# Three order changes in a fused attention and MLP training kernel: squares into the oldest output slots, one turned r tile behind the merged matrix's fourth block, two r stores moved

## The chip, the cores and the metric

The kernel runs on one core of a Trainium2 chip. The metric is the device time of one execution in microseconds (us); lower is better. A core has five engines with a queue each, and each takes its instructions in order: TensorE (PE, matmuls; PEld is its weight load), VectorE (DVE), ScalarE (ACT), GpSimd (POOL) and SyncE (SP). SP, ACT and POOL also issue DMA transfers, and an issue that waits holds up what stands behind it in the same queue. Accumulators of matmuls are in PSUM, all other tiles in SBUF.

## The reference

The reference is a transformer block with linear attention and a gated MLP, and its gradients: it returns the output and the gradients of the input and of five weight matrices. The tensors are bf16; x is 1 x 2048 x 640, there are 32 heads of 20 columns, and the MLP is 1728 wide.

```python
def _A_ref(x, wqkv, wo):
    ...
    q, k, v = qkv[0], qkv[1], qkv[2]
    phi = lambda t: jnp.where(t > 0, t + 1, jnp.exp(t)) + 1e-6
    pq, pk = phi(q), phi(k)
    kv = jnp.einsum("bhsd,bhse->bhde", pk, v)
    z = jnp.einsum("bhsd->bhd", pk)
    num = jnp.einsum("bhqd,bhde->bhqe", pq, kv)
    den = jnp.einsum("bhqd,bhd->bhq", pq, z)[..., None] + 1e-6
    o = num / den
    return (lambda x, *d: x.transpose(*d))(o, 0, 2, 1, 3).reshape(B, S, D) @ wo
...
x = A_x
h = x + _A_ref(_layernorm(x, axis=-1), A_wqkv, A_wo)
h2 = h + _B_ref(_layernorm(h, axis=-1), B_w1, B_w3, B_w2)
...
_out, _vjp = jax.vjp(_f, A_x, A_wqkv, A_wo, B_w1, B_w3, B_w2)
_grads = _vjp(grad_out)
```

## The kernel before

The 2048 rows are 16 tiles of 128 rows (index t), the 640 columns five blocks of 128 (index m or i). The order of instructions on every engine is the order of the program text: it is written out by hand, and waits between engines follow from which tile is read and written. A buffer with a tag and a number of copies is handed out in turn, and a new tile in it waits for the last reader of the old one.

*First part (to about 98 us).* The kernel forms the normalised x, the query features pq and the key features pk. Instead of kv it forms a merged matrix m = (normalised x) against pk, in five blocks: `m_part` adds matmuls (L430), `m_end` casts a finished block to SBUF with ACT (L437) and, for the first four blocks, turns it into `mT` by a DMA transpose on SP (L442). `kvT_block` (L449) multiplies mT with the value weights; for m = 2 it reads columns 240 to 400 of mT, the last 16 of which come from the fourth block. For each row tile the kernel forms r, the query features divided by their denominator: `r_prod` (POOL for tiles 0 to 7, L367), `r_red` (DVE, L374), `r_inv` (DVE) and `r_scale` (DVE, L381). `r_row` is the last three of these, and `r_head` is `r_row` and then `r_T`, which turns the tile into pqT by a DMA transpose on SP (L385). r also goes to DRAM, for the backward part: `r_store` issues that on POOL (L735).

The query tiles 0 to 3, 8 and 9 lie in one large tile (hx in the profile); tiles 4 to 7 lie in `pql`, a tag with four copies. After tile 7 the next to take a copy of it are `f2_hn(2)`, the normalised h of row tile 2 (in the place of tile 4), and the load `r_load(8)` (in the place of tile 5), issued on SP (L740).

The list in `run(...)` (from L947 on) gives the order of the end of this part. `f2_wT` makes the matrix Wp, turned by five DMA transposes on SP (L709). `f2_half` multiplies turned r with Wp into `at` (L657), adds it to x and takes the statistics on DVE; POOL forms the reciprocal root by a power (L155); `f2_hn` writes the normalised tile hn on DVE (L161); for tiles 2 and 3 PE transposes hn (L768, `trh`). `f2_m_out` stores the merged matrix's fifth block from POOL (L715).

*Middle.* The MLP, its backward part and the attention's backward part follow; the change does not touch them.

*Value gradient (about 560 to 611 us).* `obs` is an output tile of 128 x 3200, used as a ring. Gradient jobs (`grad_halves`, L1344) take slots of 320 columns in turn by a counter, ten in all: ACT casts the accumulator into the slot (L1348) and POOL stores it (L1350). Jobs 0 to 9 of the query gradient come first; `fill(1)` issues half a job. Into the last loops five "squares" are mixed, one for each block of the value weight gradient: `square` forms it (L1378), `unload` copies columns 0 to 379 with ACT and 380 to 639 with DVE (L1384) into a piece of 640 columns of obs (two slots of a job), and POOL stores it (L1455). The squares come at n = 8, 10, 12, 14 and 16 of the loop; by the first of them jobs 0 to 7 are cast and half of job 8 is issued. Accumulators of squares and of the matmuls around them (L1439, `dkv`) share three buffers.

Of the kernel before, what the change touches and what calls it, by code (L numbers as in the profile page):

```python
# [55 lines left out]
def kernel(  # L56
# [20 lines left out]
    dma, dmaT, dmaG = SY.dma_start, SY.dma_start_transpose, G.dma_start  # L77

    def rows(ap):
        return ap.rearrange("(t p) d -> p t d", p=P)  # L80
# [22 lines left out]
    r_v, pk_v, xn_v, hn_v, m_v, pq_v = rows(r_d), rows(pk_d), rows(xn_d), rows(hn_d), rows(m_d), rows(pq_d)  # L103
# [149 lines left out]
    def p1_tr(t, parts=((0, DT),)):  # L253
        xn = x_sb[:, t, :]
        for a, b in parts:
            tr = ps.tile([P, DT, P], BF16, name="tr", bufs=2)
            for c in range(a, b):
                T.transpose(tr[:, c, :], xn[:, c * P:(c + 1) * P], ident[:])

            A.copy(out=pqT[:, a:b, t * P:(t + 1) * P], in_=tr[:, a:b, :])  # L260
# [13 lines left out]
    def p1_mm(t, n0, between=None, halves=None):  # L274
        acc = p1_acc() if halves is None else None
        for j in range(2):
            p1_half(acc[:, j, 0:HD] if halves is None else halves[j][:, 0:HD], t, n0 + j * HD)
            if j == 0 and between is not None:
                between()
        return acc  # L280
# [22 lines left out]
    def phi_rest(keep=0):  # L303
        while len(held) > keep:
            held.pop(0)()

    pqs = {}
# [13 lines left out]
    def q_tile(t):  # L321
        q_home(t)
        phi(p1_mm(t, 0), pqs[t], t)
# [7 lines left out]
    def z_diag(m):  # L331
        dz[m] = hx[:, 10, m * P:(m + 1) * P]
        V.tensor_scalar(out=dz[m], in0=ident[:], scalar1=Z[:, m:m + 1], scalar2=None, op0=ALU.mult)
# [25 lines left out]
    def r_prod(t):  # L359
        for j in range(2):  # L360
            js = slice(j * HD, (j + 1) * HD)
            if t < 8:
                pr[t, j] = (p1.tile([P, HD], F32, name="pr", bufs=2) if t % 2 else
                            pf.tile([P, HD], F32, name="pr", tag="h2", bufs=2))[:]
            else:
                pr[t, j] = ps.tile([P, 512], F32, name="prp", tag="at", bufs=2)[:, 0:HD]
            (G if t < 8 else V).tensor_tensor(out=pr[t, j], in0=pqs[t][:, js], in1=Zb[:, js], op=ALU.mult)  # L367
# [4 lines left out]
    def r_red(t, js=(0, 1)):  # L372
        for j in js:
            V.reduce_sum(out=rden[:, t, j * 16:(j + 1) * 16], in_=heads(pr.pop((t, j))), axis=AX.X)  # L374

    def r_inv(t):
        V.tensor_scalar(out=rden[:, t, :], in0=rden[:, t, :], scalar1=1e-6, scalar2=None, op0=ALU.add)
        V.reciprocal(out=rden[:, t, :], in_=rden[:, t, :])

    def r_scale(t):  # L380
        V.tensor_tensor(out=heads(pqs[t]), in0=heads(pqs[t]),  # L381
                        in1=rden[:, t, :].unsqueeze(2).to_broadcast([P, H, DH]), op=ALU.mult)

    def r_T(t):
        dmaT(out=pqT[:, :, t * P:(t + 1) * P], in_=pqs[t])  # L385
# [39 lines left out]
    def m_part(m, tiles, js=(0, 1)):  # L425
        if m not in macc:
            macc[m] = [ps.tile([P, 512], F32, name="macc", tag=("m", "tr")[m % 2], bufs=2) for _ in range(2)]
        for t, j in [(t, j) for t in tiles for j in js]:
            n = HD + (m < 2) * j
            T.matmul(macc[m][j][:, 0:n], lhsT=pk_all[:, t, m * P:(m + 1) * P],  # L430
                     rhs=x_ext[:, t, j * HD:j * HD + n], start=(t == 0), stop=(t == ST - 1))

    def m_end(m, js=(0, 1)):
        mb = mbs[:, m % 4, :]
        acc = macc[m]
        for j in js:
            A.copy(out=mb[:, j * HD:(j + 1) * HD], in_=acc[j][:, 0:HD])  # L437
        if m < 2:
            A.copy(out=Z[:, m:m + 1], in_=acc[1][:, HD:HD + 1])
            z_diag(m)  # L440
        if m < DT - 1:
            dmaT(out=mT[:, :, m * P:(m + 1) * P], in_=mb)  # L442
# [13 lines left out]
    def load_w2T(a, b):  # L456
        dmaT(out=w2T[:, :, a:b], in_=B_w2[a:b, :])
# [70 lines left out]
    for t in range(ST):  # L528
        first = None
        if t < RAW:  # L530
# [11 lines left out]
            k = p1_mm(t, D, between, kh)  # L542
            act(0, 1)
            act(1, 1)
        else:
            k = p1_mm(t, D, (lambda: p1_tr(t + 1)) if t + 1 < XT_DMA else None)
# [30 lines left out]
    def r_row(t):  # L577
        r_red(t)
        r_inv(t)
        r_scale(t)  # L580

    def r_head(t):
        r_row(t)
        r_T(t)
# [24 lines left out]
    phi_rest()  # L609
    m_part(3, range(5))  # L610
    q_tile(6)
    r_head(1)
    r_prod(3)
    phi_rest()
    m_part(3, range(5, 11))
# [4 lines left out]
    phi_rest()  # L620
    m_part(3, range(11, ST))
    m_end(3)
    r_T(2)
    load_w2T(4 * P, 8 * P)
    dmaG(out=m_v[:, 1:4, :], in_=mbs[:, 1:4, :])
# [4 lines left out]
    kvT_block(1, big())  # L630
    r_row(4)
    r_prod(6)
    phi_rest()
    m_part(4, range(5, 11))
    q_tile(9)
# [308 lines left out]
    def kv3():  # L944
# [5 lines left out]
        (f2_wT, 4), (phi_rest,), (q_late, 14), (r_T, 4), (r_head, 5), (load_x, 4, 6), (r_prod, 7),  # L950
        (q_out, 10, 14), (mlp_ghh, 4),
        (q_late, 15), (w2_room,), (sig_table,), (f2_half, 0, 0), (f2_half, 1, 0), (f2_half, 2, 0), (f2_half, 3, 0), (mlp_ghh, 5),
        (f2_half, 0, 1), (r_store, 4, 5), (f2_half, 1, 1), (f2_hn, 0), (r_store, 5, 6), (f2_half, 2, 1), (f2_hn, 1),
        (f2_half, 3, 1), (f2_m_out,),
        (f2_half, 4, 0, True), (mlp_ghh, 6), (f2_half, 4, 1, True), (f2_half, 5, 0, True), (r_red, 6, (0,)), (f2_hn, 2), (f2_hn, 3),
        (f2_ht, 2), (f2_ht, 3), (load_w2T, 8 * P, 10 * P), (mlp_ghh, 7), (r_red, 6, (1,)), (r_inv, 6), (r_scale, 6),
        (r_T, 6), (f2_rest,), (r_red, 7), (r_inv, 7), (r_scale, 7), (r_T, 7), (r_store, 6, 7))
# [38 lines left out]
    for c in range(SC):  # L996
# [9 lines left out]
        for fc in range(FT):  # L1006
# [23 lines left out]
            if c == SC - 1 and fc in (1, 2, 5, 6):  # L1030
                i = (1, 2, 5, 6).index(fc)
# [339 lines left out]
    def d_acc():  # L1371
        return ps.tile([P, 2, 512], F32, name="dkv", bufs=3)

    def square(lhsT, rhs, i):

        acc = d_acc()
        for c, a, b, bank, off, first in SQ:
            T.matmul(acc[:, bank, off:off + (b - a) * DH], lhsT=lhsT[:, c, i * P:(i + 1) * P],  # L1378
                     rhs=rhs[:, c, a * DH:b * DH], start=first, stop=True, skip_group_check=True)
        return acc  # L1380

    def unload(acc, out):
        for bank, (a, b) in enumerate(((0, SPLIT_D), (SPLIT_D, H))):
            (A.copy, V.tensor_copy)[bank](out=out[:, a * DH:b * DH], in_=acc[:, bank, 0:(b - a) * DH])  # L1384

    def fill(n):
        for _ in range(n):
            next(jobs, None)
# [45 lines left out]
    for n in range(0, SC * DT, 2):  # L1434
        pair = [divmod(i, DT) for i in (n, n + 1)]
        acc = d_acc()
        for b, (c, d) in enumerate(pair):
            for k in range(DT):
                T.matmul(acc[:, b, :], lhsT=gm[:, k, d * P:(d + 1) * P], rhs=xnT[c][:, k, :], start=(k == 0),  # L1439
                         stop=(k == DT - 1))  # L1440
        for b, (c, d) in enumerate(pair):
            cs = slice(c * W, (c + 1) * W)
            pm = dx.tile([P, W], BF16, name="pm", bufs=2)
            V.tensor_scalar(out=pm[:], in0=pkT[:, d, cs], scalar1=1.0, scalar2=None, op0=ALU.min)
            V.scalar_tensor_tensor(out=g_kT[:, d, cs], in0=acc[:, b, :], scalar=gz[:, d:d + 1], in1=pm[:], op0=ALU.add,
                                   op1=ALU.mult)
        if n < 16:
            fill(1)
        if 8 <= n < 8 + 2 * DT:
            i = n // 2 - 4  # L1450
            sq = square(mN, gkv_b, i)
            k = (4, 0, 1, 2, 3)[i]
            ob = obs[:, k * D:(k + 1) * D]
            unload(sq, ob)
            dmaG(out=out2S[:, i, 2 * D:3 * D], in_=ob)  # L1455
# [21 lines left out]
    def both_grads(m, f0, f1):  # L1477

        return [(max(f0, lo) - f0, min(f1, lo + F) - f0, out[:, m, max(f0, lo) - lo:min(f1, lo + F) - lo])
                for lo, out in ((0, out4S), (F, out5S)) if max(f0, lo) < min(f1, lo + F)]  # L1480
# [60 lines left out]
    for i, (f0, f1) in enumerate(blocks):  # L1541
        n = f1 - f0
        for m in range(DT):
            last = (i, m) == (len(blocks) - 1, DT - 1)
            for a, b in ((0, n - P), (n - P, n)) if last else ((0, n),):
                c = (a + b) // 2
                halves = ((a, c), (c, b)) if i * DT + m < 6 else ((a, b),)
                out = [(x + y - a, z + y - a, to) for y, w in halves for x, z, to in both_grads(m, f0 + y, f0 + w)]
# [43 lines left out]
```

## Time and profile before

| what | us |
|---|---|
| median of 3 runs | 821.31 (820.56 to 822.07) |
| the profiled execution | 819.31 |
| its span, first to last instruction | 817.3 |
| PE busy in the span | 812.6 |
| PE busy in the window 90 to 100 | 9.98 |
| PE busy in the window 595 to 612 | 17.00 |

The granted TensorE clock is 1.00 in all windows. The span is what the trace shows; the execution's own time is 2.0 us longer. The timeline gives, for each group of like instructions that follow each other, the start in us, the time they cover, the engine, the line, the operation, what is written and read, shapes and the number; in square brackets stands how long the engine was idle just before and what ended it.

### The profile page before, as it was taken

The numbers are of one execution on the slowest core, as the hardware profiler recorded it, in microseconds if no ns is written. First come the engines' busy times: TensorE is split into PE (matmuls) and PEld (weight loads), VectorE is DVE, ScalarE is ACT, GpSimd is POOL, SyncE is SP. The second block draws the span as 40 slices with busy tenths as digits, with TensorE's granted clock in tenths as the row PEclk, the third lists the DMA queues.
The fourth block names the chain that finished last, engine by engine and source line by source line (L and its number), as shares of the span: only waits on it lengthen the run. The fifth ranks groups of instructions, "written<-read, shape, count | busy, mean of one in ns | idle before, by whom it ended". The sixth has DMA issues, their size and how long they took to land.

```text
span 817.3 us, 13571 instructions
## 1 busy us (share of the span) xinstructions
PE 812.6 (99%) x5227; PEld 495.2 (61%) x5227; DVE 444.9 (54%) x976; ACT 324.4 (40%) x607; POOL 128.6 (16%) x194
## 2 busy tenths in 40 slices
PE   9999999999999999999999999999999999999998
PEld 6777544555555555754577777777657777544444
DVE  7859997998898566300057777772565551000000
ACT  7856688665565666011122212222113442111111
POOL 2243333323222212100001111110120000000000
PEclk9999999999999999999999999999999999999999
DMA  9799899696485556999867887259995679679991
GB/s 257 210 241 283 207 264 317 203 243 175 125 211 154 169 173 168 227 263 239 242 176 182 211 198 199 58 114 180 214 184 104 122 166 255 177 179 233 239 220 38
DMA packets 334480, 159.83 MB, mean 196 GB/s; under 512 B 252304, under 2 KB 327920, under 8 KB 334416
## 3 DMA queue, kind: packets, MB, share of 16 engines
q1 hardware_dynamic: 290976, 119.37, 62.7%
q0 software_dynamic: 7008, 23.17, 8.4%
q10 hardware_dynamic: 36432, 16.42, 8.2%
q8 instruction: 41, 0.67, 0.3%
q14 instruction: 23, 0.19, 0.1%
HBM read 44.47 MB, written 53.43 MB: 120 GB/s over the span
## 4 chain that ended last, share of the span: by engine, by line
PE 98%; DVE 1%; ACT 0%; DMA 0%; POOL 0%; issue 0%
PE mm L395 21%; PE job L1344 20%; PE ghn L1131 14%; PE gxn L1495 8%; PE gw L1086 7%; PE big L268 4%; PE o L913 4%; PE o L859 3%; PE gwo L1219 3%; PE macc L430 3%; PE at L657 3%; PE gr L1188 3%; PE dkv L1439 3%; PE mm L268 1%; PE dkv L1378 1%; PE gp L395 1%
## 5 line engine op out<-in xcount | busy, mean ns | idle before, releaser
L1344 PE MATMUL job<-gb,g_q 128*128 128x496 bf16 (+3 forms) x576 | 116.8, 366 | 0.0
L1131 PEld LDWEIGHTS <-ggb 128*128 128x128 bf16 x864 | 84.5, 98 | 33.0
L395 PE MATMUL mm<-pqT,w 128*128 128x512 bf16 x405 | 93.6, 379 | 0.0
L1344 PEld LDWEIGHTS <-g_q 128*128 128x128 bf16 x576 | 55.8, 98 | 61.0
L395 PEld LDWEIGHTS <-w 128*128 128x128 bf16 x540 | 52.6, 98 | 63.0 <-issue 0.8
L1348 ACT CAST obs<-job 128x496 bf16<-128x496 f32 (+4 forms) x56 | 28.6, 511 | 136.5 <-PE job L1344 126.0
L1131 PE MATMUL ghn<-w13a,ggb 128*128 128x320 bf16 x448 | 63.5, 299 | 0.0
L1131 PE MATMUL ghn<-w13b,ggb 128*128 128x320 bf16 x416 | 61.4, 299 | 0.0
L1146 DVE SCALAR_TENSOR_TENSOR wb<-gs,hnb 128x640 f32<-128x640 bf16 x16 | 13.2, 825 | 88.1 <-ACT gs L1143 88.1
L395 PE MATMUL mm<-g2T,w2T 128*128 128x512 bf16 x240 | 59.6, 379 | 0.0
L1086 PE MATMUL gw<-hb,g 128*128 128x512 bf16 (+2 forms) x320 | 58.6, 346 | 0.0
L1086 PEld LDWEIGHTS <-g 128*128 128x128 bf16 x320 | 31.3, 98 | 26.9
L420 ACT CAST ghh<-mm 128x512 bf16<-128x512 f32 x48 | 28.1, 585 | 47.6 <-PE mm L395 41.2
L1196 POOL TENSOR_TENSOR sz<-Zb,g_h 128x640 f32<-128x640 bf16 x16 | 20.2, 1261 | 163.6 <-DVE g_h L1197 163.6
L796 ACT ACTIVATE sig<-mm 128x512 bf16<-128x512 f32 x56 | 33.7, 602 | 25.2 <-PE mm L395 21.7
L1143 ACT ACTIVATE gs<-ghn 128x640 bf16<-128x640 f32 x16 | 11.2, 703 | 77.1 <-PE ghn L1131 77.1
L395 PEld LDWEIGHTS <-w2T 128*128 128x128 bf16 x260 | 25.4, 98 | 23.4
L268 PEld LDWEIGHTS <-pqT 128*128 128x128 bf16 x320 | 30.7, 98 | 13.5 <-ACT pqT L260 0.9
L1344 PEld LDWEIGHTS <-g 128*128 128x128 bf16 x320 | 31.0, 98 | 12.8
L268 PE MATMUL big<-wqkv,pqT 128*128 128x320 bf16 x250 | 38.5, 299 | 0.2
L832 DVE TENSOR_TENSOR gate<-gate,sig 128x1024 bf16<-128x1024 bf16 x28 | 19.3, 689 | 33.8 <-ACT gate L807 31.1
L1091 ACT CAST gw2o<-gw 128x512 bf16<-128x512 f32 (+2 forms) x20 | 10.4, 519 | 65.5 <-PE gw L1086 25.5
(212 smaller groups left out, 1378.1 us busy)
## 6 DMA issues: line engine op xcount, KB each, us to landing
hh_d<-hhT SPq DMA_DIRECT2D x24, 256.0 KB, 2.8
gg_d<-gate POOLq DMA_DIRECT2D x24, 256.0 KB, 4.4
gg_d<-ghh POOLq DMA_DIRECT2D x24, 256.0 KB, 4.1
ggb<-gg_d SPq DMA_DIRECT2D x6, 896.0 KB, 5.4
ggb<-gg_d ACTq DMA_DIRECT2D x6, 832.0 KB, 5.6
ggb<-gg_d SPq DMA_DIRECT2D x2, 1728.0 KB, 12.6
x_sb<-in_A_x_dram SPq DMA_DIRECT2D x4, 640.0 KB, 5.1
pk_d<-pk_all SPq DMA_DIRECT2D x4, 640.0 KB, 5.7
```

The costliest lines, as they stand in the source:

```text
L268: T.matmul(acc, lhsT=pqT[:, c, t * P:(t + 1) * P], rhs=wqkv[:, c, n0:n0 + HD], start=(c == 0), stop=(c == DT - 1))
L395: T.matmul(acc[:], lhsT=w[:, c, fc * P:(fc + 1) * P], rhs=rhs[:, c, :], start=(c == 0), stop=(c == DT - 1))
L420: A.copy(out=ghh[n // 2][:, n % 2, :], in_=acc[:])
L430: T.matmul(macc[m][j][:, 0:n], lhsT=pk_all[:, t, m * P:(m + 1) * P], rhs=x_ext[:, t, j * HD:j * HD + n], start=(t == 0), stop=(t == ST - 1))
L657: T.matmul(at[:, 0:HD], lhsT=pqT[:, c, t * P:(t + 1) * P], rhs=Wp[:, c, j * HD:(j + 1) * HD], start=(c == 0 and not on_pe), stop=(c == DT ...
L796: A.activation(sig[:, i, :], gp[:], AF.Sigmoid)
L913: T.matmul(o2["ps"][:, 0:HD], lhsT=hhT[c][:, fc, i * P:(i + 1) * P], rhs=w2[:, fc, j * HD:(j + 1) * HD], start=(fc == 0), stop=(fc == FT - 1))
L1086: T.matmul(acc[:, 0:fw], lhsT=g2[:, t, m * P:(m + 1) * P], rhs=hb[b][:, t, 0:fw], start=(t == 0), stop=(t == ST - 1))
L1131: T.matmul(acc[:, j, 0:HD], lhsT=ggb[t // 2][:, k, lo:lo + P], rhs=rhs[:, j * HD:(j + 1) * HD], start=(k == 0), stop=(k == NG - 1))
L1344: T.matmul(acc[:, 0:n], lhsT=lhs[:, t, m * P:(m + 1) * P], rhs=rhs(t), start=(t == 0), stop=(t == ST - 1))
L1348: A.copy(out=ob, in_=acc[:, 0:n])
L1495: T.matmul(acc[:, j, 0:HD], lhsT=g, rhs=wqT[:, k, j * HD:(j + 1) * HD], start=(k == 0), stop=(k == 14))
```

## The change

- `r_head(1)` becomes `r_row(1)`, and `r_T(1)` comes after `m_end(3)`. On SP, the transpose of r tile 1 and that of the merged matrix's fourth block change places; nothing else moves in that queue.
- The store of r tile 4 moves up on POOL, to behind the products of tile 6. It is issued by a line of its own, as `r_store` is not defined yet there.
- The store of r tile 5 moves down, to behind the store of the merged matrix's fifth block.
- The five squares take the pieces 0, 1, 2, 3, 0 of obs; before they took 4, 0, 1, 2, 3.

```diff
@@ first part @@
     m_part(3, range(5))
     q_tile(6)
-    r_head(1)
+    r_row(1)
     r_prod(3)
...
     m_end(3)
+    r_T(1)
     r_T(2)
     load_w2T(4 * P, 8 * P)
...
     r_row(4)
     r_prod(6)
+    dmaG(out=r_v[:, 4, :], in_=pqs[4])
     phi_rest()
...
-        (f2_half, 0, 1), (r_store, 4, 5), (f2_half, 1, 1), (f2_hn, 0), (r_store, 5, 6), (f2_half, 2, 1), (f2_hn, 1),
-        (f2_half, 3, 1), (f2_m_out,),
+        (f2_half, 0, 1), (f2_half, 1, 1), (f2_hn, 0), (f2_half, 2, 1), (f2_hn, 1),
+        (f2_half, 3, 1), (f2_m_out,), (r_store, 5, 6),
@@ value gradient @@
             i = n // 2 - 4
             sq = square(mN, gkv_b, i)
-            k = (4, 0, 1, 2, 3)[i]
+            k = i % 4
             ob = obs[:, k * D:(k + 1) * D]
             unload(sq, ob)
             dmaG(out=out2S[:, i, 2 * D:3 * D], in_=ob)
```

## The prediction, made before the changed kernel was run

> **What bounds the kernel now.** I began with the page: the busy times and the chain that ended last.
>
> ```profile
> span 817.3 us, 13571 instructions
> PE 812.6 (99%) x5227; PEld 495.2 (61%) x5227; DVE 444.9 (54%) x976; ACT 324.4 (40%) x607; POOL 128.6 (16%) x194
> ...
> PE 98%; DVE 1%; ACT 0%; DMA 0%; POOL 0%; issue 0%
> ```
>
> TensorE (PE) is busy for all but 4.7 us (817.3 - 812.6), and the chain that ends the run is PE for 98% of the span. So time can be won only where a matmul waits. The second view is the list of waits on PE alone (engine, line, what released it: sum, times, longest).
>
> ```profile
> PE warm L468 <- DVE zero L125: 1.1, 1, 1.1
> PE k L268 <- DMA wqkv<-in_A_wqkv_dram: 0.5, 2, 0.3
> ```
>
> Both belong to the first microseconds, which the change does not touch. But matmul ends are modelled, so a short wait can hide inside a busy PE. I therefore read the timeline at each of the places the change touches, from start to start: matmuls of 320 columns follow each other every 0.136 us (ten in 1.36 us in the chain), of 512 columns every 0.216 us.
>
> First, the stores of turned r rows (L735) and the normalised tiles (hn):
>
> ```profile
> 91.99 0.59 POOL L735 DMA_DIRECT2D r_d<-pql  x1
> ...
> 94.63 0.48 DVE L374 TENSOR_REDUCE rden<-pr 128x16 f32<-128x320 f32 x1
> 94.82 0.84 PE L657 MATMUL at<-Wp,pqT 128*128 128x320 bf16 x5
> 95.18 0.82 DVE L161 TENSOR_SCALAR hn<-x_sb,ln_mv,ln_rs 128x640 bf16<-128x640 bf16 x2
> 95.69 0.82 PE L768 MATMUL trh<-ident,hn 128*128 128x128 bf16 x10
> ```
>
> The five matmuls from 94.82 are over at 94.82 + 5 x 0.136 = 95.50, and the transposes of hn start at 95.69: PE stands for 0.19 us. hn of tile 2 lies in the buffer that held tile 4's r row, so it waits for that row's store. Second, the value-gradient squares and the output slots (obs):
>
> ```profile
> 601.09 0.42 ACT L1348 CAST obs<-job 128x320 bf16<-128x320 f32 x1 [4.95 <-DMA out_dram<-obs]
> ...
> 601.41 0.48 ACT L1384 CAST obs<-dkv 128x380 bf16<-128x380 f32 x1
> ...
> 601.93 0.43 DVE L1384 CAST obs<-dkv 128x260 bf16<-128x260 f32 x1 [2.37 <-ACT obs L1384]
> ...
> 602.62 1.24 PE L1439 MATMUL dkv<-xnT,gm 128*128 128x512 bf16 x5
> ```
>
> ACT stands 4.95 us for the store of the first square, since a later cast wants half of its slot; the second square is unloaded behind it, and its accumulator is taken again by the matmuls at 602.62. They come 0.26 us after the unload's end (601.93 + 0.43 = 602.36): PE loses nothing, by 0.26 us. Third, the queue of transposes on SP:
>
> ```profile
> 67.65 2.45 SPq L385 DMA_TRANSPOSE pqT<-hx  x1
> ...
> 70.20 1.24 SPq L442 DMA_TRANSPOSE mT<-hx  x1
> ...
> 75.39 1.12 PE L449 MATMUL kv<-mT,wqkv 128*128 128x160 bf16 x15
> ```
>
> Landings come from the DMA view, asked for each issue alone (KB, us from issue to landing): the L735 store at 91.99, the first square's store at 596.89, mT's fourth block at 70.20, the third Wp transpose at 82.29.
>
> ```profile
> r_d<-pql POOLq DMA_DIRECT2D x1, 160.0 KB, 3.1
> ```
>
> ```profile
> out_dram<-obs POOLq DMA_DIRECT2D x1, 160.0 KB, 4.1
> ```
>
> ```profile
> mT<-hx SPq DMA_TRANSPOSE x1, 4.8
> ```
>
> ```profile
> Wp<-pkx SPq DMA_TRANSPOSE x1, 2.7
> ```
>
> So r's store lands at 95.1 (hn starts 0.08 later), the square's at 601.0 (the cast starts 0.09 later), mT's block at 75.0 (0.39 before its first reader at 75.39), Wp's third block at 85.0 (0.20 before the first at matmul, 85.19).
>
> **The change, part by part.** No matmul, vector operation or byte is added or removed; PE's order is the same. It moves three DMA issues and five slot numbers.
>
> *Store of r tile 4, earlier.* It goes from POOL at 91.99 to behind the products of tile 6 (issued 73.06 for 1.53 us), where it waits for the scaling of tile 4 on DVE (74.31 + 0.97 = 75.28) and takes 0.59 us of POOL. Queued behind it on POOL is the product of tile 7, which starts at 84.16: 8.3 us of cover, cost 0. What it frees: hn of tile 2 no longer waits for a landing at 95.1. DVE is next late, since its queue holds the reduction until 94.63 + 0.48 = 95.11: gain 95.18 - 95.11 = 0.07 us. Bounds: 0, and 0.28, the whole of the gap (0.19) and of the one behind the next five matmuls (96.35 + 5 x 0.216 = 97.43 to 97.52, 0.09). I take 0.07.
>
> What it costs where it goes: 160 KB join a full stretch (DMA share 1.00 between 75 and 90). Over the run POOL's queue moved 23.17 MB in 8.4% of 817.3 us, so 160 KB are 0.49 us of all 16 engines. It would land near 75.3 + 3.1 = 78.4, before the first Wp transpose is issued (79.67), with the 640 KB x load between them. The third Wp has 0.20 us to spare, so the loss lies between 0 and, if 0.49 us passed through whole, 0.29. I take 0, nearer to the row: this transpose took 2.7 us where the least of the five took 2.6, so its issue and not the backlog sets it.
>
> The Trainium skill (DMA: Bandwidth & Descriptors, section SWDGE vs HWDGE vs iDMA) says that the two kinds of queue feed different internal queues of each DMA engine, which takes them in turn. By that rule a transpose under way would give up every other turn to the store, and its delay ends with the store's own 0.49 us; the sum would then hold up to +0.29. The rows are harsher: the transpose at 67.65 ran beside a 480 KB POOL store and took 7.1 us, where the one at 71.54 took 4.0.
>
> *Store of r tile 5, later.* From POOL at 93.12 to behind the store of mT's fifth block (95.30 + 0.58 = 95.88). The next POOL work is the power for tile 4 at 100.22: 3.7 us of cover. Its buffer is next written by a load that SP issues at 111.92; landing near 95.9 + 3.0 = 98.9 leaves 13 us. Both stores also leave the row of power operations on POOL (92.60, 93.73), but DVE's hn of tile 1 (93.44) follows its own previous step at 93.38 at once, so nothing is won. Cost 0.
>
> *r_T(1) behind mT's fourth block, on SP.* Each issue keeps its work; the two change places. mT's source is cast by 65.71 + 0.75 = 66.46, so it can go out at 67.65 instead of 70.20. In r_T(1)'s place (7.1 us) it would land at 74.75 rather than 75.0; if it kept its own 4.8 us, at 72.45. kv starts at 75.39 behind matmuls, so 0 is won here and the margin grows from 0.39 to between 0.64 and 2.9 us. r_T(1) lands near 75.0; its reader, tile 1's at matmuls, starts at 85.87 (85.19 + 5 x 0.136): 10.9 us of cover. r_T(2) and all behind keep their places. Cost 0.
>
> *Squares in slots 0 to 3, then 0.* The cast no longer waits for the square's store: ACT and DVE run some 2 us sooner at 601, and PE gains 0, as it did not wait. The new waits: squares 0 to 3 now go where jobs 0 to 7 were, whose last store is issued at 592.81, 13 us before square 3's unload (606.39). Square 4 needs square 0's store, landed at 601.0, before its unload at 608.88: 7.9 us. Cost 0.
>
> Sum: the profiled execution took 819.31 us (span 817.3 and 2.0 around it), so 819.31 - 0.07 = 819.24. The median of the three runs is 821.31, 2.00 above the profiled execution, and the page does not say where those 2.00 us go.
>
> **What the landings add.** An estimate: the four L735 stores of this profile took 3.1, 3.0, 2.1 and 5.3 us. hn starts at DVE's own pace if the landing takes at most 3.03 (so that it is back at DVE by 95.11); the mean of what lies above it is (0.07 + 0 + 0 + 2.27) / 4 = 0.59 us. The change takes that wait away. For the median I so take 821.31 - 0.59 = 820.7. The other two (slack of 0.26 and 0.39 us) get nothing in it.
>
> **The rivals.**
>
> *All of the 2.00 us are such waits* (hn's store, the square's store, mT's block). For it: of the three landings one decides a start and two come within 0.4 us; the rows of these transfers spread widely (mT 3.3 to 7.4 us, obs stores 2.0 to 6.5). A landing of 5.3 at hn costs 2.2 us, of 6.5 at the square 6.5 - 4.1 - 0.26 = 2.1, of 7.4 at mT 7.4 - 4.8 - 0.39 = 2.2. Against: the profile shows none of it. Then 821.31 - 2.00 - 0.07 = 819.2.
>
> *The moved store delays Wp: slower.* The 480 KB beside the 67.65 transpose went with 3.1 us more (7.1 against 4.0). If 160 KB did as much to the third Wp transpose, PE would stand before the first at matmul for 3.1 - 0.20 = 2.9 us: 824.2. It is slower by over 0.2% from a delay of 1.84 us (0.20 + 1.64). Against: a third of the bytes, and the x load between them.
>
> *It does nothing*: PE is full and every piece lies in cover. 821.2.
>
> **How the numbers follow.** 0.2% is 1.64 us, about what a measurement of this kernel can tell from no change. Chances: the forecast 0.38, nothing 0.12, all waits gone 0.34, Wp delayed 0.16. The first two are within 0.2%: same 0.50; faster 0.34; slower 0.16. The time is 820.7, the forecast's. The range goes from 818.9, just below the 819.2 of the rival, to 822.8, past which lies most of the slower case (its partial stalls, such as 0.49 or 1 us, are inside). The forecast's own range is 820.0 to 821.6.
>
> **What would show it.** In the profile after: hn of tile 2 starts right behind the reduction on DVE, and the gap before the hn transposes falls to about 0.12 us; the wait of obs L1348 on its store is gone and the ACT cast comes near 599; mT's fourth block is issued at about 67.6 and r_T(1) at about 70.2; the at matmuls follow the queries without a gap at 85.2. I am wrong if PE stands before the first at matmul, if the store on POOL holds up tile 7's product, or if repeated runs fall by more than 1.6 us while the profile shows no wait removed.

## The result, and the profile after

The changed kernel took 819.35 us (median of 14 runs, 819.10 to 820.21), the kernel before 820.74 us in the 14 runs beside it (819.39 to 822.24). The ratio is 0.9982, 95% interval 0.9974 to 0.9991: 1.5 us less, between 0.7 and 2.1. That is clear of no change, though just inside the 0.2% that the prediction called the same.

The profiled execution of the changed kernel took 819.31 us, to a hundredth what the profiled one of before took. From the page, its span, the busy times and the chain:

```profile
span 817.4 us, 13576 instructions
...
PE 811.9 (99%) x5227; PEld 494.9 (61%) x5227; DVE 445.1 (54%) x976; ACT 324.7 (40%) x607; POOL 129.0 (16%) x194
...
PE 98%; DMA 1%; ACT 0%; SPq 0%; issue 0%
```

The list of PE's waits after:

```profile
PE warm L468 <- DVE zero L125: 1.1, 1, 1.1
PE k L268 <- DMA wqkv<-in_A_wqkv_dram: 1.1, 2, 0.6
PE tr L258 <- ACT x_sb L479: 0.2, 1, 0.2
PE mm L395 <- DMA pqT<-hn: 0.2, 1, 0.2
```

One execution against one execution so shows no gain at all: the loads of the first microseconds cost 0.6 us more here (1.1 against 0.5), and the list has a wait that was not in that of the kernel before, for the DMA transpose of hn. Three timelines show what the change did. Around hn:

```profile
94.53 0.48 DVE L374 TENSOR_REDUCE rden<-pr 128x16 f32<-128x320 f32 x1
...
94.79 0.84 PE L659 MATMUL at<-Wp,pqT 128*128 128x320 bf16 x5
94.93 0.97 DVE L161 TENSOR_SCALAR hn<-x_sb,ln_mv,ln_rs 128x640 bf16<-128x640 bf16 x2
95.19 0.58 POOL L717 DMA_DIRECT2D m_d<-hx  x1
...
95.47 0.93 PE L770 MATMUL trh<-ident,hn 128*128 128x128 bf16 x10
...
95.77 0.54 POOL L737 DMA_DIRECT2D r_d<-pql  x1
...
96.24 1.24 PE L395 MATMUL mm<-g2T,w2T 128*128 128x512 bf16 x5
...
97.64 0.61 PE L395 MATMUL mm<-pqT,w 128*128 128x512 bf16 x2 [0.15 <-DMA pqT<-hn]
```

From the end of the at matmuls to the first mm there were 96.35 - 95.50 = 0.85 us; now there are 96.24 - (94.79 + 0.68) = 0.77. That is 0.08 less, about the 0.07 of the prediction, though in another way: the gap before the hn transposes is gone, and the ten transposes take 0.77 us instead of 0.66. But the next matmuls begin at 97.64, where 96.24 + 5 x 0.216 = 97.32 would do: 0.32 us of wait in place of 0.09. Around the second square, ACT no longer waits for a store:

```profile
599.07 0.42 ACT L1350 CAST obs<-job 128x320 bf16<-128x320 f32 x1 [2.73 <-PE job L1346]
599.44 0.47 ACT L1386 CAST obs<-dkv 128x380 bf16<-128x380 f32 x1
...
599.95 0.43 DVE L1386 CAST obs<-dkv 128x260 bf16<-128x260 f32 x1 [0.23 <-ACT obs L1386]
```

The square is unloaded at 600.38 (before, 602.36), and PE takes its accumulator at 602.77: the slack of 0.26 us has become 2.4. And the first square's store, which landed in 4.1 us in the profile of before, took longer in this execution (DMA view, that issue alone, at 597.10):

```profile
out_dram<-obs POOLq DMA_DIRECT2D x1, 160.0 KB, 5.4
```

With the old slots, an estimate: 5.4 us instead of 4.1 would have cost 5.4 - 4.1 - 0.26 = 1.0 us of PE. On SP, the merged matrix's block goes out sooner:

```profile
67.85 2.46 SPq L442 DMA_TRANSPOSE mT<-hx  x1
70.42 2.54 SPq L385 DMA_TRANSPOSE pqT<-hx  x2
```

### The profile page after: what moved, and what is told of

The parts are those of the page before. It is cut to its first block, busy times and chain, and to the rows that moved or that the text cites. A ratio compares the mean times of both kernels' runs of the same rounds, so it can differ in the third digit from the quotient of the medians.

```text
span 817.4 us, 13576 instructions
## 1 busy us (share of the span) xinstructions
PE 811.9 (99%) x5227; PEld 494.9 (61%) x5227; DVE 445.1 (54%) x976; ACT 324.7 (40%) x607; POOL 129.0 (16%) x194
## 4 chain that ended last, share of the span: by engine, by line
PE 98%; DMA 1%; ACT 0%; SPq 0%; issue 0%
PE mm L395 21%; PE job L1346 20%; PE ghn L1133 14%; PE gxn L1497 8%; PE gw L1088 7%; PE big L268 4%; PE o L915 4%; PE o L861 3%; PE gwo L1221 3%; PE macc L430 3%; PE gr L1190 3%; PE dkv L1441 3%; PE at L659 3%; PE mm L268 1%; DMA wqkv<-in_A_wqkv_dram 1%; PE dkv L1380 1%
```

## The experiments

Each kernel was timed beside the kernel before on the same chip; times are medians, "before" is that of its group. The first is the kernel before itself and the last differs from the changed kernel; all others differ from the kernel before by the edit shown.

| kernel | us | before | ratio (95% interval) |
|---|---|---|---|
| before, again | 820.43 | 820.56 | 0.9998 (0.9990 to 1.0007) |
| squares alone | 819.54 | 820.56 | 0.9989 (0.9980 to 0.9998) |
| turn alone | 820.35 | 820.56 | 1.0001 (0.9993 to 1.0009) |
| stores alone | 820.37 | 820.56 | 0.9999 (0.9990 to 1.0008) |
| turn and stores | 821.15 | 821.09 | 1.0003 (0.9993 to 1.0014) |
| squares and stores | 819.75 | 821.09 | 0.9985 (0.9977 to 0.9994) |
| squares, worse slots | 821.31 | 821.09 | 1.0005 (0.9994 to 1.0016) |
| stores swapped | 821.00 | 821.09 | 1.0002 (0.9991 to 1.0013) |
| cast later | 820.24 | 821.52 | 0.9987 (0.9974 to 0.9999) |
| stores late | 822.27 | 821.52 | 1.0014 (0.9999 to 1.0030) |
| squares and turn | 820.23 | 821.52 | 0.9985 (0.9973 to 0.9996) |
| changed, two stores later still | 820.30 | 821.52 | 0.9986 (0.9975 to 0.9997) |

### One part at a time

**The kernel before, again** (no edit).

> The kernel before, again. Every theory: ratio 1.000 to the kernel before, within 0.1%; it shows the noise of the comparison. Its executions should spread over some 3 us as before (819.4 to 822.2). The profile may catch another execution than the first one: if landings decide, the three places (hn of tile 2 after the r store, the cast behind the first square's store, kv after mT's fourth block) are where PE then stands.

It came out the same, 0.9998. Its profile caught another execution (820.0 us), in which mT's fourth block landed late:

```profile
PE kv L449 <- DMA mT<-hx: 0.9, 1, 0.9
```

The block was issued at 70.41 and took 5.8 us, so it landed at 76.2; kv began at 76.23, where 75.19 (ten matmuls from 73.83, 0.136 us each) would have done. PE stood there for 0 us in one profiled execution of this program and for 1.0 us in the other.

**Squares alone.**

```diff
-            k = (4, 0, 1, 2, 3)[i]
+            k = i % 4
```

> Only the squares' slots are changed (0, 1, 2, 3, 0). Theory (the store of r tile 4 holds up hn): within 0.3 us of the kernel before, with its spread of 3 us. Rival A (the cast that waits for the first square's store is what costs in repeated runs): 1.0 to 1.5 us faster, 819.3, with a spread of 1 us. Rival B (mT's fourth block): no change.

0.9989: 0.9 us, and the interval leaves out no change. That is rival A's direction, a little under its size, with a spread of 1.6 us (819.06 to 820.64) where 1 was expected; the kernel before beside it spread over 3.7 us (819.01 to 822.74).

**Turn alone.**

```diff
-    r_head(1)
+    r_row(1)
...
     m_end(3)
+    r_T(1)
     r_T(2)
```

> Only the transpose of r tile 1 is put behind mT's fourth block. Theory (r store of tile 4): within 0.3 us of the kernel before. Rival A (squares): no change. Rival B (mT's fourth block comes late for kv in repeated runs): 1.0 to 1.5 us faster, 819.3, with a spread of 1 us.

1.0001: rival B falls as the main cause. The wait at kv is there, but it shows in one of the nine profiles without the turn.

**Stores alone.**

```diff
     r_prod(6)
+    dmaG(out=r_v[:, 4, :], in_=pqs[4])
...
-        (f2_half, 0, 1), (r_store, 4, 5), (f2_half, 1, 1), (f2_hn, 0), (r_store, 5, 6), (f2_half, 2, 1), (f2_hn, 1),
-        (f2_half, 3, 1), (f2_m_out,),
+        (f2_half, 0, 1), (f2_half, 1, 1), (f2_hn, 0), (f2_half, 2, 1), (f2_hn, 1),
+        (f2_half, 3, 1), (f2_m_out,), (r_store, 5, 6),
```

> Only the stores of r tiles 4 and 5 are moved. Theory (hn of tile 2 waits for the landing of r tile 4's store): 0.6 to 1.4 us faster, 819.4 to 820.1, with a narrower spread. Rivals A and B: within 0.3 us of the kernel before.

0.9999: the theory of the prediction falls as the main cause; the interval leaves it 0.8 us at most. The profile of this run, which has the old slots, shows in its place what squares cost. PE's rows around the second and third squares:

```profile
604.01 0.49 PE L1379 MATMUL dkv<-gkv_b,mN 128*128 128x140 bf16 x6
604.88 0.81 PE L1440 MATMUL dkv<-xnT,gm 128*128 128x512 bf16 x3 [0.38 <-DVE obs L1385]
```

The six short matmuls of a square take 0.34 us (602.28 to 602.62 in the profile of before), so PE could go on at 604.35 and stood 0.53 us. It waited for DVE's copy of the second square. That copy was late because ACT had first stood 5.70 us for the cast that it has ahead of its own share of the square:

```profile
603.57 0.43 ACT L1349 CAST obs<-job 128x320 bf16<-128x320 f32 x1 [5.70 <-DMA out_dram<-obs]
```

### The squares against the rest

**Turn and stores, old slots** (the two edits above together).

> The changed kernel without the new slots: the turn and both stores moved, squares still in 4, 0, 1, 2, 3. Theory now (the squares' slots alone bring the gain, since the cast behind the first square's store sometimes holds PE): ratio to the kernel before 0.9995 to 1.0005, its spread as wide as before. Rival (the three parts help together: each alone is hidden by the others' waits): 0.9985 or below.

1.0003: without the new slots nothing is left of the gain.

**Squares and stores, no turn.**

> Squares and both stores, without the turn. Theory (squares alone): 0.9985 to 0.9990. Rival (the turn adds, as a wait of 1.04 us of PE for mT's fourth block was seen in one profile of the kernel before): slower than the changed kernel by 0.3 us or more, 0.9990 or above, and the profile may show PE waiting at kv.

0.9985, at the better end of the band expected for the theory; PE did not wait at kv in its profile. The turn adds nothing that can be measured.

**Squares in worse slots.**

```diff
-            k = (4, 0, 1, 2, 3)[i]
+            k = (0, 4, 1, 2, 3)[i]
```

> Only the slots: squares to 0, 4, 1, 2, 3, so that the second square's unload itself waits for the store of job 8 (issued near 599.8, landing 3.4 us later, 603.2) and ends near 604.1, while PE wants that accumulator at 602.6. Theory (a late unload of a square stops PE through the three dkv buffers): PE stands 1.5 us there in the profile and the kernel is 0.5 to 1.5 us slower than before, 1.0006 to 1.0018. Rival (the slots act in another way, such as by traffic, and PE does not hang on the unload): no wait of PE there, within 0.0005 of the kernel before.

The mechanism held: the second square's unload on ACT came at 603.68 and on DVE at 604.19, and PE stood from 603.42 (603.08 + 0.34) to 604.67.

```profile
603.08 0.49 PE L1378 MATMUL dkv<-gkv_b,mN 128*128 128x140 bf16 x6
604.67 2.32 PE L1439 MATMUL dkv<-xnT,gm 128*128 128x512 bf16 x10 [1.09 <-DVE obs L1384]
```

That is 1.25 us, yet the time rose by 0.4 us only (1.0005, 0.9994 to 1.0016). By the time alone this is the rival's band; it is the wait in the profile that speaks against the rival. The step from the new slots (0.9985 to 0.9989) to these is 0.0016 to 0.0020, or 1.3 to 1.6 us, which fits the 1.25. It suggests that in repeated runs the kernel before already pays a good part of such a wait, though its first profile shows none.

**Stores swapped.** Tile 5's store at the place of tile 4's, tile 4's behind the power of tile 2.

```diff
-        (f2_half, 0, 1), (r_store, 4, 5), (f2_half, 1, 1), (f2_hn, 0), (r_store, 5, 6), (f2_half, 2, 1), (f2_hn, 1),
+        (f2_half, 0, 1), (r_store, 5, 6), (f2_half, 1, 1), (f2_hn, 0), (f2_half, 2, 1), (r_store, 4, 5), (f2_hn, 1),
```

> Only the stores of r tiles 4 and 5 change places on POOL, so that tile 4's is issued behind the power of tile 2 (about 1 us later, landing near 96.3 to 97). Theory of the prediction (hn of tile 2 starts when this store lands, and PE waits for hn): PE stands 1 to 2 us before the transposes of hn and the kernel is 1 to 2 us slower, 1.0012 to 1.0024. Rival (hn has cover in repeated runs, which is why moving the store up brought nothing): no change, within 0.0005.

1.0002, and hn of tile 2 began at 94.99, right behind DVE's reduction. This did not test what it was meant to: tile 4's store was issued at 94.11 and landed 2.5 us later, at 96.6, so hn did not wait for it. The first of the two stores, now that of tile 5, was issued at 91.85 and landed 3.1 us later, at 94.95, as in the kernel before. So hn seems to take the buffer whose store is issued first, and not strictly the next in turn. Its profile shows PE standing 0.91 us for the second square (605.13 to 606.04) with a store that took 5.2 us.

### The wait and what stands behind it

**Cast later.** Old slots, but half a job is issued behind the second square instead of before it. Its matmuls on PE move with its cast.

```diff
-        if n < 16:
+        if n < 16 and n != 10:
             fill(1)
...
             dmaG(out=out2S[:, i, 2 * D:3 * D], in_=ob)
+        if n == 10:
+            fill(1)
```

> Squares in their old slots (4, 0, 1, 2, 3), but the second half of job 8 is issued behind the second square instead of before it, so ACT unloads that square first and then waits for the first square's store. The wait itself stays. Theory (the wait costs because the unload behind it in ACT's queue holds a dkv accumulator): the same gain as the new slots, 0.9985 to 0.9992, no wait of PE at dkv however late the store lands. Rival (the wait or the traffic of the slots itself is what costs): 0.9996 to 1.0004.

0.9987, the gain of the new slots, though the interval (0.9974 to 0.9999) just touches the rival's band. The store took 5.7 us here and the cast still waits for it, but the unload stands ahead of it now:

```profile
598.61 0.47 ACT L1384 CAST obs<-dkv 128x380 bf16<-128x380 f32 x1 [2.06 <-PE dkv L1378]
603.06 0.42 ACT L1348 CAST obs<-job 128x320 bf16<-128x320 f32 x1 [3.98 <-DMA out_dram<-obs]
```

PE went on without a gap from the third square:

```profile
602.70 0.50 PE L1378 MATMUL dkv<-gkv_b,mN 128*128 128x140 bf16 x6
603.03 2.32 PE L1439 MATMUL dkv<-xnT,gm 128*128 128x512 bf16 x10
```

By the slack in the profile of before, a landing of 5.7 us in the old order would have cost 5.7 - 4.1 - 0.26 = 1.3 us, an estimate. It is the unload queued behind the wait that costs, not the wait.

**Both stores late.** Both behind the power of tile 2 on POOL.

```diff
-        (f2_half, 0, 1), (r_store, 4, 5), (f2_half, 1, 1), (f2_hn, 0), (r_store, 5, 6), (f2_half, 2, 1), (f2_hn, 1),
+        (f2_half, 0, 1), (f2_half, 1, 1), (f2_hn, 0), (f2_half, 2, 1), (f2_hn, 1), (r_store, 4, 5), (r_store, 5, 6),
```

> Both stores of r tiles 4 and 5 on POOL behind the power of tile 2, so that whichever buffer hn of tile 2 takes is freed late: issue near 94.1, landing 2.5 to 3.1 us later, 96.6 to 97.2. Theory (hn of tile 2 waits for that landing and PE for hn; in the kernel before the landing is just in time): PE stands 1.3 to 2 us before the hn transposes; 1.0012 to 1.0024. Rival (no such dependence): no wait of PE there, 0.9995 to 1.0005.

PE stood as expected. The first store was issued at 94.12 and landed 2.3 us later, at 96.4; hn began at 96.47, the transposes at 96.97 instead of 95.45 (94.77 + 0.68): 1.52 us.

```profile
PE trh L768 <- DVE hn L161: 1.4, 1, 1.4
```

1.0014, with an interval (0.9999 to 1.0030) that holds the 1.5 us and just holds none. So hn does hang on that store; where the kernel before puts it, it lands in time or up to 0.5 us late.

**Squares and turn, no stores.**

> Squares and the turn, without the stores. Theory (the stores win 0.1 us at hn of tile 2 and lose 0.2 to 0.6 us to a later transpose of hn of tile 1): as good as the changed kernel or better, 0.9975 to 0.9985; in the profile the matmuls behind the hn transposes start with at most 0.1 us of wait, and hn of tile 1 lands in 2.6 to 2.7 us. Rival (the stores are part of the gain): slower than the changed kernel, 0.9990 or above.

0.9985: as good as the changed kernel within the intervals. The details missed: hn of tile 1 took 3.2 us to land, not 2.6 to 2.7, and PE stood 0.56 us before the hn transposes (95.40 to 95.96) and 0.14 behind (97.68 to 97.82). In the seven profiles with both stores in their old places PE stood 0.0 to 0.6 us before the hn transposes, in the four with the stores moved as in the change 0. But from the end of the at matmuls to the first matmul on the turned hn of tile 1 there were 1.9 to 2.5 us in those seven (mean 2.1) and 2.15 to 2.55 in those four (mean 2.35): the moved stores take the one wait away and give at least as much back behind it.

**The changed kernel with two stores later still.**

```diff
-        (f2_half, 3, 1), (f2_m_out,), (r_store, 5, 6),
+        (f2_half, 3, 1),
...
-        ... (r_red, 6, (0,)), (f2_hn, 2), (f2_hn, 3),
+        ... (f2_hn, 2), (r_red, 6, (0,)), (f2_hn, 3),
...
-        (r_T, 6), (f2_rest,), (r_red, 7) ...
+        (r_T, 6), (f2_rest,), (f2_m_out,), (r_store, 5, 6), (r_red, 7) ...
```

> The changed kernel, with the store of the merged matrix's fifth block and that of r tile 5 further down (behind the statistics of tiles 4 and 5, near 100), and hn of tile 2 on DVE before the reduction of tile 6. Theory (both stores beside the transpose of hn of tile 1 make it land late): it lands in 2.3 to 2.6 us, PE stands less than 0.1 us at hn and at the matmuls behind; 0.3 to 0.7 us below the changed kernel, 0.9973 to 0.9980. Rival (the transpose is late for another reason): a wait of 0.3 to 0.7 us stays at those matmuls, 0.9980 to 0.9990.

The edit also puts hn of tile 2 on DVE before the reduction of tile 6. The waits moved as the theory said at the matmuls (the transpose of hn took 2.6 us, and no wait is left there), but the ten hn transposes still took 0.85 us (95.71 to 96.56; before, 0.66), with a stop between tiles 2 and 3. 0.9986: no better than the others that have the new slots, and in the rival's band of time. It cannot be told from the changed kernel, so there is no version here that beats it.

## Why the prediction was right or wrong

The time, 819.35, lies in the range and on the side forecast, by 1.5 us where 0.6 (821.31 to 820.7) was expected. That is luck in good part: the gain came from another part than the one counted, and 820.7 is what the kernel before itself took in the 14 runs (820.74). One of the prediction's signs of being wrong was a fall of more than 1.6 us with no wait removed in the profile. It came close: 1.5 us, with both profiled executions at 819.31.

*"ACT and DVE run some 2 us sooner at 601, and PE gains 0, as it did not wait"* is the step that failed; the slack of 0.26 us was read rightly, and then the spread of the landing was given nothing there ("The other two (slack of 0.26 and 0.39 us) get nothing in it"). In the seven profiles of kernels with the old slots and the old order, the first square's store took 3.5, 3.6, 3.7, 3.7, 4.1, 4.8 and 5.2 us. PE stood 0 in the first five, 0.53 in that of the stores alone (4.8) and 0.91 in that of the swapped stores (5.2): by these two, each us above 4.3 is a us of PE. In the seven other profiles the same store took 3.1 once and 5.3 to 5.7 six times. Over all fourteen the mean above 4.3 is 8.5 / 14 = 0.6 us, an estimate of what the old slots cost on average; by the seven of the old order alone it is 1.4 / 7 = 0.2. Measured were 0.9 us (squares alone) to 1.2 (squares with one other part). So the mechanism is shown, by the slots and by the later cast, but the waits seen in the profiles do not add up to the whole gain.

*"The change takes that wait away", 0.59 us for hn's store:* a misjudged size. The stores alone gave 0.9999 (0.9990 to 1.0008). The estimate rested on one landing of 5.3 us among four, and that is another store, the one at 115.8. The store of r tile 4 itself landed in 2.7, 2.9, 3.1, 3.1, 3.2, 3.4 and 3.5 us in the seven profiles that have it in its old place; the mean above 3.03 is 1.15 / 7 = 0.16 us in place of 0.59. The wait exists (both stores late: 1.5 us), but the move gains 0.08 us in the profile and loses 0.23 to a wait that the prediction did not have: the store of the merged matrix's fifth block and that of r tile 5 now leave POOL back to back (95.19 and 95.77) beside the DMA transpose of hn of tile 1. It takes 3.3 us in the changed kernel where it took 2.6, and matmuls wait for it, 0.32 us here and 0.67 in the kernel with turn and stores (96.28 + 1.08 = 97.36 to 98.03), whose transpose took 3.4:

```profile
98.03 0.82 PE L395 MATMUL mm<-pqT,w 128*128 128x512 bf16 x3 [0.51 <-DMA pqT<-hn]
```

With both stores moved on, the transpose took 2.6 us again and the wait was gone. The cost of 0 for the later store of r tile 5 was worked out for POOL and the buffer alone, and not for what the transfer runs beside. The Trainium skill (DMA: Bandwidth & Descriptors, section SWDGE vs HWDGE vs iDMA) has the DMA engines take turns between the two kinds of queue. By that rule, two stores of 0.49 us each could delay a transpose by up to 0.98 us, an estimate; the 0.7 to 0.8 us of the traces lie within it. That contention alone lengthens it is not shown, as it also took 3.2 us twice with the stores in their old places.

*The turn:* "it would land at 74.75", or at best 72.45. mT's block was issued at 67.85, as foreseen, but took 7.1 us, as r tile 1's transpose had in that place, and landed at 74.95, just where it had landed (75.0). A gain of 0 fits the measured ratio (turn alone, 1.0001); of the nine profiles without the turn one shows the wait at kv, of the five with it none.

*The rivals:* "all waits gone" (819.2) was the nearest in time, with the part of the square's store right and those of hn's store and of mT's block not borne out by the times. "The moved store delays Wp" did not happen: the at matmuls start at 85.17 right behind the queries (84.62 + 4 x 0.136 = 85.16).

## What to carry to other kernels

Where one engine is full, a single profile can miss waits because the landings happened to be in time. Read each place where a DMA landing decides, write down the slack, and take the landing's spread over several profiles of that same place, not of like transfers elsewhere. A wait in an in-order queue is priced by what stands behind it: here the cast could wait 4 us at no cost once the unload stood ahead of it. Before a store is moved to a free spot of its queue, look at which transfers it will run beside.

## What was not expected of the hardware

The landing of one and the same 160 KB store, that of the first square, ranged from 3.1 to 5.7 us over fourteen profiled executions. It goes with where the store falls against a transpose on SP (into wqT). These are the transpose's rows before and after; the stores were issued at 596.89 and 597.10:

```profile
597.42 4.13 SPq L1299 DMA_TRANSPOSE wqT<-in_A_wqkv_dram  x1
```

```profile
595.82 4.33 SPq L1301 DMA_TRANSPOSE wqT<-in_A_wqkv_dram  x1
```

In the three profiles where the store was issued 0.3 to 0.5 us ahead of the transpose, it landed in 3.1 to 4.1 us. In the eight with a landing of 4.8 to 5.7 us it was issued 1.1 to 1.7 us behind the start of the transpose, and it landed about 2.3 us after the end of the transpose's row, with old slots and with new. In the last three it was issued 0.7 to 1.1 us behind and landed in 3.5 to 3.7 us, and there the transpose's row is the longest (4.9 to 5.1 us, elsewhere at most 4.6). No run moved one of the two, so that the transpose is the cause is not shown.

PE also waits at a place that the change does not touch: at gkvT, for DMA transposes into tri, 0 in the profiles of before and after, and 1.9 us in that of the swapped stores:

```profile
PE gkvT L1395 <- DMA tri<-tri: 1.9, 1, 1.9
```

Three more of the fourteen profiles list this wait, with 0.6 to 0.7 us. No run here tried to remove it.
